# Retention and an x·cos(x) MLP on one core: the first units by head halves, two middle units in coarser chunks

## The chip, the cores and the metric

The kernel runs on one core of a Trainium2 chip. The metric is the device time of one execution in microseconds, and the time of a kernel is the median of its runs. An engine carries out its own instructions in order: TensorE (PE; PEld are its weight loads), VectorE (DVE), ScalarE (ACT), GpSimd (POOL) and SyncE (SP), which issues most of the DMAs.

## The reference

Eight batches of eight heads, 576 positions, head size 64. Attention without a softmax, with a decay by distance, then an MLP on all 4608 tokens:

```python
scores = scale * np.matmul(q, k.transpose(0, 1, 3, 2))
gamma = 1.0 - 2.0 ** (-5.0 - np.arange(H, dtype=np.float32))
Dmat = np.where(rel >= 0, gamma[:, None, None] ** rel[None, :, :], 0.0)
attn = np.matmul(scores * Dmat[None], v)
x = attn.transpose(0, 2, 1, 3).reshape(B * S, H * D)      # 4608 x 512
h = x @ w_in                                              # 512 -> 2048
out = (h * np.cos(h)) @ w_out                             # 2048 -> 512
```

## The kernel before

**Units.** The attention is cut into units `(b, g)`: batch `b`, all eight heads, tokens 256·g to 256·g+255. The last 64 tokens of four batches each make the units `(0, 2)` and `(1, 2)`. The order of units is (0,0), (1,0), (0,1), (1,1), (2,0), (3,0), (2,1), (3,1), (4,0), ..., and two of them (two batches, the same g) make one block of 512 tokens for the MLP, nine blocks in all.

**One unit.** SP loads k, q and v of the unit as float32 into `stgk`, `stgq`, `stgv` (`load`, L484). They are cast to bf16 into `natk`, `qnat`, `natv` (`unit`, L521 for the products with the decay tables `wq`, `wv`; L475 or L474 for the plain casts), with tokens on the partitions. k and q are then transposed into `kt` and `qt`: in blocks 0 and 1 (`NOXBAR`) by TensorE and a copy out of PSUM (`tpe`, L545, copies L474 and L475), in the later ones by a pair of transposing DMAs on SP (`txb`, L560). `scores` multiplies kt and qt within a chunk of tokens on TensorE in four concurrent 64x64 lanes (`emit_lanes`, L591), VectorE multiplies by the triangular mask into `pt` (L630). `states` sums k times v over the chunks in PSUM (`st`), ScalarE copies the sum out (`snap`, into `sba`, `sbb`, `sbr`), and `outputs` adds pt times v and q times the sum of the earlier chunks; two copies bring that into `xt`, the block's MLP input.

A unit is worked in chunks of 64 or of 128 tokens. `fine(u)` says which: fine units (chunks of 64, from batch 2 on, without those in `COARSE`) are loaded in two halves of 128 tokens (256-byte rows), need scores of 64 columns, two pt products and four snaps. The others are loaded whole (512-byte rows), with scores of 128 columns, four pt products and two snaps. Both have the same number of matmuls for the scores and the intra-chunk outputs.

**The first units.** (0,0) and (1,0) are loaded with `fast=True`: q before k before v, each tensor whole, with VectorE casting q, ScalarE and POOL casting a half of k each, and the transposes' copies shared by ScalarE and VectorE. w_in comes in four quarters (`load_w`, issued on POOL, cast to bf16 by the DMA), each gated on a staged tile: quarter 0 on q of (0,0), quarter 2 on q of (1,0), 1 and 3 on k of (1,0). Unit (0,1) is gated on quarter 2. w_out comes in four quarters gated on q of (1,1).

**The MLP.** `mlp1` makes one slice `f` of 128 hidden units for a block or half a block (4 matmuls, L795), ScalarE takes the cosine (L803), VectorE the product into `gt` (L806). `wino2` does the second product in a form with seven instead of eight half-products: VectorE sums of gt and of w_out (L839, L861, L867), TensorE groups `P1`, `P2`, `P6`, `P5`, `P7`, `P3`, `P4` of 16 matmuls (L930), copies and sums (L474, L919), stores (L818).

**The order.** No loop order is written out. `graph` adds tasks with costs in ns and due times (`prio`), and `Graph.run` plans all engines on these costs ahead of time; the resulting order of each engine's instructions is fixed in the program, and each instruction waits for what it needs. `plan` says with which session of which unit the states of which chunk go. Where the planner expects a gap on TensorE in the first 45 us, `warm` puts fillers in: matmuls of a tile of ones (`bk<-one`, L419) whose result is not used. [...]

Of the kernel before, what the change touches and what calls it, by code (L numbers as in the profile page):

```python
# [6 lines left out]
ALU = mybir.AluOpType  # L7
# [12 lines left out]
NT = 72  # L20
# [309 lines left out]
class Kernel:  # L330
# [8 lines left out]
    COARSE = ((2, 0), (3, 0))  # L339
# [138 lines left out]
    def load(self, which, u, rows, gate, fast):  # L478

        stg = self.staged[which, u] = Buf("stg" + which)  # L480
        src = self.src["qkv".index(which)]
        for i, (p0, n, o, ny, b, r0) in enumerate(rows):
            at, w = (b * H * S + r0) * D, ny * D
            self.one("sp", 500, lambda e, p0=p0, n=n, o=o, w=w, at=at: e.dma_start(  # L484
                ap(self.at(stg), 1024, p0, n, o, [w, H], [1, w]), bass.AP(src, at, [[w, n], [S * D, H], [1, w]])),
                r=gate, w=[(stg, i)], sem=lambda i=i: f"{which}{stg.slot}_{i}", dma=1840 if ny == 2 else 600 * n // 64, tail=720 if fast else 1800)
        return stg

    def unit(self, u, fast=False, gate=()):
# [3 lines left out]
        todo = [("k", "natk", "kt"), ("q", "qnat", "qt"), ("v", "natv", None)]  # L493
        for which, nat, dst in [todo[i] for i in ((1, 0, 2) if fast else (0, 1, 2))]:
            if rem:
                rows = [(64 * (b % 2), 64, 512 * (b // 2), 1, 4 * u[0] + b, 512) for b in range(4)]
            elif fine:
                rows = [(0, 128, 512 * y, 1, u[0], 256 * u[1] + 128 * y) for y in range(2)]
            else:
                rows = [(0, 128, 0, 2, u[0], 256 * u[1])]  # L500
            stg = self.load(which, u, rows, gate, fast)
            nb = t[nat] = Buf(nat)
            for y in range(2):
                rs = [(stg, i) for i in ((y,) if fine else range(len(rows)))]
# [9 lines left out]
                if which == "k":  # L514
                    eng = ("act", "pool")[y] if fast else "pool"
                    self.copy(eng, {"act": 520, "dve": 610, "pool": 580}[eng], out, inp, rs, [(nb, y)])
                else:
                    tab, key = (self.WV, "wv") if which == "v" else (self.WQ, "wq")
                    col = 32 if rem else 40 * fine + 16 * u[1] + 8 * y
                    eng = "dve" if fast and which == "q" else "pool"  # L520
                    self.one(eng, 610 if eng == "dve" else 1030, lambda e, out=out, inp=inp, tab=tab, col=col, hs=hs: e.tensor_tensor(  # L521
                        out(), inp(), ap(tab, NT, 0, 128, col, *hs, [0, D]), ALU.mult),
                        r=rs + [(key,)], w=[(nb, y)], port=eng == "pool")
            if dst:
                t[dst] = Buf(dst)
                if self.where(u) in self.NOXBAR:
                    for y in range(2):
                        self.tpe(nb, 512 * y, [(y,)], t[dst], (y,), ("act", "dve")[y] if fast else "act")
        if self.where(u) not in self.NOXBAR:
            self.txb(u)  # L530

    def fine(self, u):
        return u[1] < 2 and u[0] >= 2 and u not in self.COARSE

# [4 lines left out]
    def tpe(self, src, off, rk, dst, wk, eng):  # L539
        bk = Buf("bk")  # L540

        def mm(e):
            tb = self.at(bk).ap().bitcast(BF16)
            for c in range(4):
                inst = e.transpose(tb[:, c * 128:c * 128 + 128],  # L545
                                   ap(self.at(src), 1024, 0, 128, off + 128 * c, [1, 128]), self.IDN.ap())
# [6 lines left out]
        self.copy(eng, dur, lambda: ap(self.at(dst), 1024, 0, 128, off, [1, 512]),  # L553
                  lambda: self.at(bk).ap().bitcast(BF16)[:, 0:512], [(bk,)], [(dst,) + wk])

    def txb(self, u):
# [7 lines left out]
        self.G.add("sp", 2600, parts, dma=3000)  # L564
# [3 lines left out]
    def emit_lanes(self, name, prio, phases, alloc=()):  # L568

        parts, t, n = [], 200, 0  # L570
        for lanes, reads, writes, after in phases:
            lanes = {q: list(v) for q, v in lanes.items() if v}
            order, at = [], dict.fromkeys(lanes, 0.0)
            while any(lanes.values()):
                q = min((q for q in lanes if lanes[q]), key=lambda q: at[q])
                cols, f = lanes[q].pop(0)
                at[q] += cols / 2.4 + 2.5
# [8 lines left out]
            t += max(at.values())  # L586
# [6 lines left out]
    def scores(self, u, prio, todo, split, extra=(), join=None):  # L593
# [5 lines left out]
        for cc in range(1 if rem else 2):  # L599
# [16 lines left out]
            reads = [(x, y) for x in (kt, qt) for y in range(2)]  # L616
# [20 lines left out]
        for i, more in enumerate(extra):  # L637
# [3 lines left out]
            self.emit_lanes("ses=%d.%d" % u, prio + (split or 1000 * (i + 1)), [alone])  # L641
# [200 lines left out]
    def wino2(self, j, base, span):  # L842
# [80 lines left out]
        for n, p in enumerate((1, 2, 6, 5, 7, 3, 4)):  # L923
            l, rr, keys, bank, first = spec[p]
            halves = last and p == 4
            for q in range(2):
# [6 lines left out]
                self.one("pe", 8 * 109, mm, r=keys(0) + keys(1) if halves else keys(q),  # L933
# [159 lines left out]
```

## Time and profile before

| | us |
|---|---|
| median of 3 runs | 291.48 (290.73 to 293.96) |
| the profiled execution | 292.03 |
| its span, first to last instruction | 290.3 |
| TensorE busy | 280.2 (97%) |
| VectorE busy | 209.8 (72%) |
| ScalarE busy | 167.3 (58%) |
| GpSimd busy | 99.7 (34%) |

How to read the lines of the profile: a row of the timeline has its start, its length, engine, line, operation, tile written <- tiles read, shapes, the number of instructions in the row, and in brackets the engine's idle time before it and what ended that. In the DMA lines the last number is the time from issue to landing. In the slices, each digit is the busy share of one fortieth of the span, in tenths. The granted clock of TensorE is full throughout.

### The profile page before, as it was taken

The page shows a single profiled execution, that of the slowest core. Times are in us where ns is not written, and L with a number is a line of the kernel's source. Part 1 is how long each engine was busy: PE and PEld are TensorE (multiplying, and loading weights), DVE is VectorE, ACT ScalarE, POOL GpSimd, SP SyncE. Part 2 cuts the span into 40 slices and gives each one's busy share as a digit, 9 for nine tenths or more (in the row PEclk, how much of TensorE's full clock was granted, in tenths as well). Part 3 has the DMA queues.
Part 4 walks back from the last instruction along what each step waited for, and adds up shares of the span by engine and source line. Part 5 has one row for each costly group of instructions (what it writes and reads, how often), then busy time and mean ns, then how long its engine had stood idle before and what let it go on. Part 6 is the DMA issues. An engine that isn't in the chain of part 4 may idle for free.

```text
span 290.3 us, 9132 instructions
## 1 busy us (share of the span) xinstructions
PE 280.2 (97%) x3848; PEld 192.5 (66%) x3848; DVE 209.8 (72%) x352; ACT 167.3 (58%) x309; POOL 99.7 (34%) x126
## 2 busy tenths in 40 slices
PE   6799999999999999999999999999999999999996
PEld 2566577887864587458566666666666666666685
DVE  3777769999837882897688676878577847667633
ACT  5359786563358634874864766656554483544520
POOL 5451960366650644355174344441430000000000
PEclk9999999999999999999999999999999999999999
DMA  7999899999999999999999999989923000300223
GB/s 200 268 217 281 203 173 219 293 190 197 186 243 199 209 196 248 207 217 281 194 197 181 211 261 212 153 227 197 175 46 146 3 3 0 147 0 0 75 108 108
DMA packets 133127, 49.86 MB, mean 172 GB/s; under 512 B 105440, under 2 KB 128992, under 8 KB 133088
## 3 DMA queue, kind: packets, MB, share of 16 engines
q1 hardware_dynamic: 128576, 44.84, 75.0%
q0 software_dynamic: 4224, 4.19, 9.1%
q8 instruction: 30, 0.49, 0.7%
q10 hardware_dynamic: 288, 0.26, 0.3%
q14 instruction: 9, 0.07, 0.1%
HBM read 36.70 MB, written 9.44 MB: 159 GB/s over the span
## 4 chain that ended last, share of the span: by engine, by line
PE 81%; issue 4%; DVE 4%; DMA 3%; POOL 3%; ACT 2%; SPq 1%; DVEq 0%; POOLq 0%
PE bk L795 37%; PE bk L930 36%; PE bk L591 6%; DMA stgk<-in_k_dram 3%; PE st L591 2%; POOL natv L521 2%; DVE gt L806 2%; ACT cb L803 1%; SPq L484 1%; DVE s L861 1%; DVE pt L630 1%; PE bk L545 1%; POOL win L775 0%; DVE s L867 0%; POOL natk L475 0%
## 5 line engine op out<-in xcount | busy, mean ns | idle before, releaser
L803 ACT ACTIVATE cb<-bk,cpi 128x512 bf16<-128x512 f32 (+1 forms) x168 | 103.5, 627 | 71.0 <-PE bk L795 70.6
L795 PE MATMUL bk<-xt,win 128*128 128x512 bf16 (+1 forms) x672 | 140.5, 349 | 0.6 <-DVE pt L630 0.4
L806 DVE TENSOR_TENSOR gt<-bk,cb 128x512 bf16<-128x512 f32 (+1 forms) x168 | 100.7, 611 | 51.4 <-ACT cb L803 48.4
L795 PEld LDWEIGHTS bk<-xt,win 128*128 128x128 bf16 x672 | 63.9, 98 | 44.0 <-DVE pt L630 0.7
L521 POOL TENSOR_TENSOR qnat<-stgq,wq 128x512 bf16<-128x512 f32 x32 | 33.7, 1065 | 35.2 <-DMA stgq<-in_q_dram 15.0
L521 POOL TENSOR_TENSOR natv<-stgv,wv 128x512 bf16<-128x512 f32 x36 | 38.0, 1069 | 19.0 <-DMA stgv<-in_v_dram 7.4
L475 POOL CAST natk<-stgk 128x512 bf16<-128x512 f32 x34 | 20.2, 611 | 55.9 <-DMA stgk<-in_k_dram 40.3
L930 PE MATMUL bk<-wout,s 128*128 128x256 bf16 x288 | 36.3, 273 | 0.0
L930 PE MATMUL bk<-tw,s 128*128 128x256 bf16 x288 | 35.9, 273 | 0.0
L930 PE MATMUL bk<-wout,gt 128*128 128x256 bf16 x288 | 35.6, 273 | 0.0
L630 DVE TENSOR_TENSOR pt<-bk,tr 128x512 bf16<-128x512 f32 x48 | 30.2, 682 | 4.4 <-PE st L591 2.2
L930 PEld LDWEIGHTS bk<-tw,s 128*128 128x128 bf16 x288 | 28.0, 98 | 7.2
L930 PEld LDWEIGHTS bk<-wout,s 128*128 128x128 bf16 x288 | 27.5, 98 | 6.7
L930 PEld LDWEIGHTS bk<-wout,gt 128*128 128x128 bf16 x288 | 27.7, 98 | 5.4
L919 DVE TENSOR_TENSOR os<-bk,sn 128x512 f32<-128x512 f32 (+1 forms) x28 | 18.5, 664 | 15.0 <-PE bk L930 15.0
L474 ACT ACTIVATE sn<-bk 128x512 f32<-128x512 f32 (+1 forms) x29 | 16.3, 568 | 19.3 <-PE bk L930 19.3
L474 ACT ACTIVATE sba<-st 128x256 bf16<-128x256 f32 x36 | 13.2, 385 | 14.3 <-PE st L591 14.2
L474 ACT ACTIVATE xt<-bk 128x512 bf16<-128x512 f32 x33 | 19.9, 655 | 1.6 <-PE bk L591 1.6
L930 PE MATMUL bk<-tw,gt 128*128 128x256 bf16 x144 | 18.5, 273 | 0.0
L930 PEld LDWEIGHTS bk<-tw,gt 128*128 128x128 bf16 x144 | 13.9, 98 | 4.3
L861 DVE TENSOR_TENSOR s<-gt 128x1024 bf16<-128x1024 bf16 x18 | 15.4, 862 | 0.4
L867 DVE TENSOR_TENSOR s<-gt,s 128x1024 bf16<-128x1024 bf16 x18 | 14.4, 806 | 0.1
(59 smaller groups left out, 171.0 us busy)
## 6 DMA issues: line engine op xcount, KB each, us to landing
out_dram<-os SPq DMA_DIRECT2D x16, 512.0 KB, 4.2
stgk<-in_k_dram SPq DMA_DIRECT2D x20, 256.0 KB, 5.1
stgq<-in_q_dram SPq DMA_DIRECT2D x20, 256.0 KB, 4.9
stgv<-in_v_dram SPq DMA_DIRECT2D x20, 256.0 KB, 5.3
stgq<-in_q_dram SPq DMA_DIRECT2D x6, 512.0 KB, 6.9
stgk<-in_k_dram SPq DMA_DIRECT2D x6, 512.0 KB, 7.7
stgv<-in_v_dram SPq DMA_DIRECT2D x6, 512.0 KB, 7.7
win<-in_moe_w_in_dram POOLq DMA_DIRECT2D x4, 512.0 KB, 8.2
```

Of the source, the lines that this page charges most:

```text
L474: return self.one(eng, dur, lambda e: e.activation(dst(), src(), AF.Copy), r=r, w=w, **kw)
L475: return self.one(eng, dur, lambda e: e.tensor_copy(dst(), src()), r=r, w=w, port=eng == "pool", **kw)
L521: self.one(eng, 610 if eng == "dve" else 1030, lambda e, out=out, inp=inp, tab=tab, col=col, hs=hs: e.tensor_tensor(out(), inp(), ap(tab, ...
L591: return lambda e: e.matmul(out(), lhs(), rhs(), start=start, stop=True, skip_group_check=True)
L630: self.one("dve", 610, lambda e, r=r, b=b, pt=pt: e.tensor_tensor(ap(self.at(pt), 1024, 0, 128, 512 * r, [64 * ny * ny, 8 // ny // ny], [1 ...
L795: inst = e.matmul(ap(self.at(bk), 512, 0, 128, 0, [1, n]), ap(self.WIN, 4 * DFF, 0, 128, c * DFF + 128 * f, [1, 128]), ap(self.at(xt), 204 ...
L803: self.one("act", 70 + n, lambda e: e.activation(ap(self.at(cb), TB, 0, 128, 0, [1, n]), ap(self.at(bk), 512, 0, 128, 0, [1, n]), AF.Sin, ...
L806: self.one("dve", 75 + n / 0.96, lambda e: e.tensor_tensor(ap(self.at(gt), NF * TB, 0, 128, f * TB + 256 * h0, [1, n]), ap(self.at(bk), 51 ...
L861: self.one("dve", 610, lambda e, i=i, q=q, x=x, y=y, op=op: e.tensor_tensor(sv(i, q), x(), y(), op), r=r + late, w=[(S_[i, q],)], port=Tru ...
L867: self.one("dve", 610, lambda e, i=i, q=q, x=x, y=y, op=op: e.tensor_tensor(sv(i, q), x(), y(), op), r=r + late, w=[(S_[i, q],)], port=Tru ...
L919: self.one("dve", 610 if m == 1 else 345, lambda e, i=i, b=b: e.tensor_tensor(view(h, c, i, m), flat(self.at(b), 0, m), flat(self.at(sn[na ...
L930: inst = e.matmul(place(bank, tt), l(f, tt), rr(f), stop=True, skip_group_check=True, start=(first and f == 0 and tt < len(bank)))
```

## The change

Five edits in one:

- `swift` takes the place of `unit(..., fast=True)` for (0,0) and (1,0), and is used for (0,1) as well. It loads, casts and transposes each tensor by head halves (q and k: every second head; v: the first or last four), in the order q, k, q, k, v, v. For (0,1) VectorE casts q (POOL did) and ScalarE copies all transposes. The first scores phase of a unit reads only the first halves. w_in's gates are on the second halves (`GATE`).
- `COARSE` now has (2,1) and (3,1) too: chunks of 128 tokens, loads of whole tiles.
- Fine units load and cast k and v by token halves, and q after them (`ORDER`).
- `plan` moves states to other sessions: the units from (2,0) to (3,1) carry the next unit's first state in their output session, (4,0) (`LINK`) the double set.
- The costs that the planner goes by are set anew (lane sessions, transposing DMAs, due times of the extra sessions).

```diff
-    COARSE = ((2, 0), (3, 0))
+    COARSE = ((0, 0), (1, 0), (0, 1), (1, 1), (2, 0), (3, 0), (2, 1), (3, 1))
...
     def fine(self, u):
-        return u[1] < 2 and u[0] >= 2 and u not in self.COARSE
+        return u[1] < 2 and u not in self.COARSE
...
+        for which, ys in self.ORDER if fine else [(x, (0, 1)) for x in "kqv"]:
...
+    def swift(self, u, gate=()):
...
+        def part(which, a):
+            stg, nb, w = stgs[which], t[nats[which]], 2 * D
+            h0, hn = (4 * a, 1) if which == "v" else (a, 2)
+            at = ((u[0] * H + h0) * S + 256 * u[1]) * D
+            self.one("sp", 500, lambda e: e.dma_start(
+                ap(self.at(stg), 1024, 0, 128, 512 * a, [w, 4], [1, w]),
+                bass.AP(self.src["qkv".index(which)], at, [[w, 128], [hn * S * D, 4], [1, w]])),
+                r=gate, w=[(stg, a)], sem=lambda: f"{which}{stg.slot}_{a}", dma=920, tail=1800 if u[1] else 720)
...
+            eng = self.SWIFTENG[u][which][a]
+            if which == "k":
+                self.copy(eng, {"act": 520, "dve": 610, "pool": 580}[eng], out, inp, [(stg, a)], [(nb, a)])
+            else:
...
+            if which != "v":
+                self.tpe(nb, 256 * a, [(x,) for x in range(a + 1)], t[which + "t"], (a,), self.SWIFTENG[u][which + "t"][a], (512, 2))
+
+        for which, a in self.SWIFTORDER:
+            part(which, a)
...
-        self.G.add("sp", 2600, parts, dma=3000)
+        self.G.add("sp", 2600, parts, dma=3400)
...
-        parts, t, n = [], 200, 0
+        parts, t, n = [], 240, 0
...
-                at[q] += cols / 2.4 + 2.5
+                at[q] += cols / 2.4 + 5
...
-            t += max(at.values())
+            t = max([t] + [parts[i][0] + 200 for i in after if not isinstance(i, Task)]) + max(at.values())
...
-            reads = [(x, y) for x in (kt, qt) for y in range(2)]
+            reads = [(x, y) for x in (kt, qt) for y in range(cc + 1 if u in self.FAST else 2)]
...
+    FAST = ((0, 0), (1, 0), (0, 1))
+    ENG1 = dict(q=("dve", "dve"), k=("act", "pool"), v=("pool", "pool"), qt=("act", "dve"), kt=("act", "dve"))
+    ENG2 = dict(q=("dve", "dve"), k=("pool", "pool"), v=("pool", "pool"), qt=("act", "act"), kt=("act", "act"))
+    SWIFTENG = {(0, 0): ENG1, (1, 0): ENG1, (0, 1): ENG2, (1, 1): ENG2}
+    SWIFTORDER = (("q", 0), ("k", 0), ("q", 1), ("k", 1), ("v", 0), ("v", 1))
+    GATE = (1, 1, 1, 1)
+    RIDE = (4,)
+    LINK = 8
+    ORDER = (("k", (0,)), ("v", (0,)), ("k", (1,)), ("v", (1,)), ("q", (0, 1)))
+
+    def plan(self, seq):
+
+        p = {}
+        for n in range(16):
+            if n > self.LINK and n % 2:
+                p[n] = [[[(n + 1, 0), (n, 3)]], [], [[(n + 1, 1), (n + 2, 0)]]]
+            elif n > self.LINK:
+                p[n] = [[[(n, 2), (n + 1, 1)]], [], [[(n, 3), (n + 1, 2)]]]
+            elif self.fine(seq[n]):
+                p[n] = [[[(n, 0)]], [[(n, 1)], [(n, 2)]], [[(n, 3)]]]
+            elif n in self.RIDE:
+                p[n] = [[[(n, 0)]], [], [[(n, 1)]]]
             else:
...
+                p[n] = [[[]], [[(n, 0)]], [[(n, 1)]]]
+        for n in range(4, self.LINK):
+            if n > 4:
+                p[n] = [[[]], [], p[n][2]]
+            p[n][2][0] += [(n + 1, 0)]
+        n = self.LINK
+        p[n] = [[[(n, 1), (n + 1, 0)]], [[(n, 2), (n + 1, 1)]], [[(n, 3), (n + 1, 2)]]]
...
-            self.load_w("win", x, [(st[which, (min(x, 1), 0)], 0)], pr)
-        self.unit((0, 1), gate=[("win", 2)])
+            self.load_w("win", x, [(st[which, (min(x, 1), 0)], self.GATE[x])], pr)
+        if (0, 1) in self.FAST:
+            self.swift((0, 1), [("win", 2)])
```

## The prediction

> **What bounds the kernel now.** First the page's totals and its slices:
>
> ```profile
> span 290.3 us, 9132 instructions
> PE 280.2 (97%) x3848; PEld 192.5 (66%) x3848; DVE 209.8 (72%) x352; ACT 167.3 (58%) x309; POOL 99.7 (34%) x126
> PE   6799999999999999999999999999999999999996
> DMA  7999899999999999999999999989923000300223
> ```
>
> TensorE is busy 97% of the span, and thin only in the first two slices and the last. But a busy row counts pipelines and fillers. I added up columns instead, from the program's order: columns over 2.4 per ns, a fourth of that for 64x64 tiles, nothing for fillers. That is 250.7 us of real matmul work. So some 40 us of the span are not work: by the timeline's starts about 14 are lost by 20 us, 5 more by 45, 7 more between 45 and 140, 4 more after that. What an edit to the first units can give lies in the first 45 us.
>
> The timeline of the head:
>
> ```profile
> 1.13 3.68 PE L419 MATMUL bk<-one 128*128 128x512 bf16 x9 [1.13 <-DVE lg L445]
> 5.33 0.95 POOL L775 DMA_DIRECT2D win<-in_moe_w_in_dram  x1 [2.23 <-DMA stgq<-in_q_dram]
> 6.71 0.59 PE L419 MATMUL bk<-one 128*128 128x512 bf16 x2
> 9.23 2.48 DVE L630 TENSOR_TENSOR pt<-bk,tr 128x512 bf16<-128x512 f32 x4 [0.61 <-PE bk L591]
> 14.03 1.03 PE L795 MATMUL bk<-xt,win 128*128 128x256 bf16 x8
> 14.72 0.60 POOL L475 CAST natk<-stgk 128x512 bf16<-128x512 f32 x1 [3.14 <-DMA stgk<-in_k_dram]
> 20.01 0.64 PE L591 MATMUL bk<-pt,natv 64*64 64x128 bf16 x32
> 21.06 6.70 PE L795 MATMUL bk<-xt,win 128*128 128x256 bf16 x52
> ```
>
> Unit (0,0) reaches its first MLP matmul at 14.03, unit (1,0) its output matmuls at 20.01, and from 21.06 MLP matmuls follow one another. The DMA issues of the first microseconds give the landings:
>
> ```profile
> stgq<-in_q_dram SPq DMA_DIRECT2D x1, 512.0 KB, 4.2
> win<-in_moe_w_in_dram POOLq DMA_DIRECT2D x1, 512.0 KB, 8.1
> ```
>
> q lands at 0.80 + 4.2 = 5.0; by the same view k at 6.8, v at 8.6, q of (1,0) at 10.4, its k at 14.66 (the weights share the engines), its v at 16.5; w_in's first quarter at 5.33 + 8.1 = 13.4. So whole tiles come 1.8 us apart, a half 0.9.
>
> The timeline behind it, where TensorE is patched with fillers and short gaps:
>
> ```profile
> 27.21 1.16 POOL L475 CAST natk<-stgk 128x512 bf16<-128x512 f32 x2 [8.38 <-DMA stgk<-in_k_dram]
> 32.36 0.38 PE L419 MATMUL bk<-one 128*128 128x512 bf16 x1
> 33.92 0.40 PE L545 MATMUL bk<-idn,natk 128*128 128x128 bf16 x4 [0.25 <-DVE pt L630]
> 34.52 0.40 PE L545 MATMUL bk<-idn,natk 128*128 128x128 bf16 x4 [0.20 <-DVE pt L630]
> 36.92 0.21 PE L591 MATMUL bk<-qt,sba 64*64 64x128 bf16 x1 [0.20 <-issue]
> 44.77 0.61 PE L795 MATMUL bk<-xt,win 128*128 128x256 bf16 x4 [0.37 <-DVE pt L630]
> ```
>
> From 21.06 to the first wino2 group at 42.10 are 21.0 us, and what stands there costs 18.3 back to back (72 MLP matmuls of 256 columns at 0.109, 32 of 512 at 0.216, 32 transposes at 0.053, scores 0.56, states 0.23, an output session 1.06). So 2.7 us are holes.
>
> Last, the later attention sessions and the queues that feed them:
>
> ```profile
> 74.71 1.04 POOL L521 TENSOR_TENSOR natv<-stgv,wv 128x512 bf16<-128x512 f32 x1 [4.24 <-DVE s L867]
> 79.42 2.76 SPq L560 DMA_TRANSPOSE kt<-natk  x1
> 82.23 1.31 SPq L560 DMA_TRANSPOSE qt<-qnat  x1
> 85.96 0.45 PE L591 MATMUL bk<-qt,kt 64*64 64x64 bf16 x32
> 100.69 0.44 PE L591 MATMUL bk<-qt,kt 64*64 64x64 bf16 x32 [0.54 <-POOL natv L521]
> ```
>
> The scores of (2,1) start at 85.96, just as its transposed q lands (82.23 + some 4.4 of the transposes' landing). Sessions are set right behind their data, and one of them pays 0.54.
>
> **The change part by part.**
>
> *Head, (0,0) and (1,0): 0.9 us worse.* In halves, at the landing rate above, q's first half is there at 4.2, k's at 5.0, then 5.9, 6.8, v at 7.7 and 8.6. The last byte comes no sooner. VectorE takes q at 5.9 to 6.6; the second scores need k's second half (POOL 7.1 to 7.7, transposes, VectorE's copy to 8.6) and start at 8.7. Four pt products of 0.65 follow, but the new order puts the cast of (1,0)'s first q half between the third and the fourth, so the last ends at 11.2 (11.7 before) and xt is done at 13.6. This 0.4 us is not collected: w_in's first quarter now waits for q's second half, 0.9 later, and so lands at 14.3. The MLP starts at 14.35 instead of 14.03. (On POOL the cast of k's second half is queued behind that waiting issue; k lands at 6.8, so it loses 0.3, which is in the 7.1.) Unit (1,0): k's second half lands at 14.6 as before, and the transposes queued behind eight MLP matmuls bring the pt products to 17.8 and the outputs to 20.5 (20.0 before). Four MLP matmuls fewer stand ahead of them (16 for 20: 0.44). Together 0.5 + 0.44. If w_in lands as early as before, this is a gain of 0.7; if VectorE waits for q of (1,0) in front of the last pt, the loss is 1.6.
>
> *Unit (0,1), 21 to 42 us: 1.6 better.* Its loads wait for w_in's third quarter as before, which lands at much the same time (its issue moves from 10.8 to 11.3, behind the same first quarter). k landed at 27.1, q at 28.9, v at 30.5; by halves, q first, both q and k are whole at 28.9 and v again at 30.5. What is saved is POOL: two q casts of 1.05 go to VectorE, where MLP products are queued behind them; the first q half lands near 26.2, about when its turn comes, so they do not wait. natv ends at about 31.8 (33.05 before), the first scores come 2 us sooner, the outputs 1.2. In the new order 48 and 36 MLP matmuls of 256 columns stand in this stretch where 44 and 28 stood, so with the four missing ahead of it eight more (0.87) are done by the first wino2 group. I walked through the stretch with the durations above and found 1.1 us of holes (two fillers of 0.2, waits of 0.3 to 0.4 for kt and pt) instead of 2.7. Bounds: all 2.7 gained, or nothing.
>
> *42 to 51 us: nothing.* Unit (1,1) is loaded whole as before, POOL issues w_out and casts behind the same q landing, and VectorE's four pt end the wait at 44.77.
>
> *(2,1) and (3,1) in 128-token chunks: 0.85 worse.* The order's columns add up to 251.5 us instead of 250.7: scores and outputs are twice as wide. The rows agree: 32 scores of 128 columns take 0.58 to the next start, of 64 columns 0.27. This lies on TensorE itself, nothing hides it. VectorE gets four pt more (2.7 us), ScalarE four snaps fewer (1.5). VectorE is 55 to 79% busy from 80 to 100 us and covers them; uncovered they cost 2.7.
>
> *Loads and K, V by halves: 0.25 better.* Between k of (2,0) at 46.8 and the transposes of (4,0) at 99.55 SP sends 6 whole tiles, 21 halves, four pairs of transposes, two stores. After: 12 whole, 10 halves, the same pairs, three stores. Eleven halves at 1.16 (nine in the 10.4 us up to 99.55) go, six tiles at 1.8 and a store of 1.0 come: the transposes start 1.0 sooner, q lands at 105.8 (the added store, queued on SP ahead of them, has its data from some 84 us on). The stall of 0.54 goes, because these scores no longer carry states of (4,0). But q of every later unit is now behind V: two halves and two casts, 4.4 us. In the traced run the scores of (4,0) to (7,0) come 7 to 13 us after q's landing, so that is hidden, except that the planner now sets sessions earlier: by columns (4,0) at 82.4 instead of 89.3, at 107 us. The margin is 1.2 there, 3 at (3,1) and (5,0), and between 2.7 and -0.7 at (2,1). I take 0.3 for stalls, with 4.9 as the upper end (below).
>
> *Tail.* The last 130 rows of TensorE's order are the same.
>
> Sum: +0.9 - 1.6 + 0.85 - 0.54 + 0.3 = -0.1. The profiled execution took 292.03 (span 290.3 and 1.7 around it), so 291.9 for such a one; against the median of the runs, 291.48, it is **291.4**.
>
> **The rivals.**
>
> *The data do come sooner: 288.4.* w_in is in time, the first units lose nothing, all holes from 21 to 42 close (2.7), and the 0.7 around 44.77 as well: -3.4, and -0.54 + 0.85. For it: every filler there marks missing work, and POOL does lose 2.1 us. Against it: the last byte of each unit lands no sooner, and VectorE's pt row of 2.48 stays.
>
> *Sessions set too early: 296.0, slower.* TensorE's queue is in order. In POOL's order both q casts of (2,1) stand behind those of (3,0), in the stretch where POOL waited 4.24 for VectorE. By the cast at 76.4, q would land at 82, and scores are due at 81.3. One more such wait ahead of it makes that 86.2, a stall of 4.9 instead of 0.3. It decides from the point where transposed q lands after 81.3. For it: the margin is the smallest of all. Against it: DMA alone would have q there at 78.6.
>
> *The first fillers are too few: 293.5.* Nine fillers start 0.43 apart, the later pair 0.21: TensorE runs at half rate first, with the granted clock shown full all along. The order now has seven fillers, to 4.1 us, then a pause to 5.0. If that leaves it at half rate up to the MLP, the outputs of (0,0) take 1.05 more (0.7 of it under w_in's landing), transposes and 16 MLP matmuls up to (1,0)'s outputs some 1.7 more: 2.1 in all. [...] Against it: single fillers and transposes follow from 5.0 on.
>
> **How the numbers follow.** 1% (2.9 us) is about what a measurement of this kernel can tell from no change. Chances: the forecast 0.53 (290.0 to 293.2), the sooner data 0.20, the early sessions 0.17, the fillers 0.10. Faster by over 1% is most of the second (0.17), slower most of the third and a little of the fourth (0.18), the rest is within 1%. The range reaches to 288.6 and 294.8, into both outer cases.
>
> **What would show it.** Right: the first MLP matmul at 14.2 to 14.5, the long MLP row from about 21.5, the first wino2 group still near 42 with nine f done instead of seven, no wait for natv near 100. Wrong: that row from 20.5, or transposes of weights twice as far apart before 14 us, or a wait of over 1 us on kt, qt or natv between 60 and 110.

## The result

The kernel after has a median of 292.89 us (291.77 to 294.83, 22 runs), the kernel before, run beside it, 291.42 (290.36 to 293.96, 22 runs). The ratio is 1.0046, with a 95% interval of 1.0027 to 1.0065: 1.34 us slower by the ratio. The forecast was no change that can be measured, 291.4. 292.89 lies within its range, but the change made the kernel slower by more than the uncertainty of this measurement, which is 0.2% to each side and not the 1% that the prediction reckoned with. That the number is near is luck: of its five terms the largest did not come, and a sixth stood at nothing.

The profiled execution of after took 291.97 (span 290.2), 0.9 below its median, that of before 292.03, 0.6 above its own. So the two traces, laid side by side, show no loss at all: where the time went had to come from stages and from further kernels. The page's totals of after, and the slices of the granted clock:

```profile
span 290.2 us, 9057 instructions
PE 280.9 (97%) x3813; PEld 192.9 (66%) x3813; DVE 211.5 (73%) x358; ACT 166.3 (57%) x305; POOL 96.8 (33%) x124
PEclk9799999999999999999999999999999999999999
```

The second digit of PEclk is new: the granted clock was full throughout in the profile of before. By windows of 3.4 us (columns: PE, PEld, DVE, ACT, POOL busy with their counts, then the granted clock, DMA share, GB/s):

```profile
4.26:7.66 3.40, 1.57 (x15) 0.79 (x14) 1.12 (x2) 1.71 (x3) 0.78 (x1) 1.00 1.03 282
7.66:11.08 3.42, 3.22 (x44) 1.53 (x44) 2.62 (x5) 0.00 (x0) 2.84 (x4) 0.50 1.20 277
11.08:14.49 3.41, 2.75 (x80) 1.69 (x79) 2.11 (x5) 1.79 (x4) 0.81 (x1) 1.00 1.19 249
```

TensorE is busy 46% of the window up to 7.66 and then runs at half rate for 3.4 us. One of the prediction's signs of being wrong, transposes twice as far apart before 14 us, is there: four of them take 0.61 at 8.51, where four took 0.40 before. The timeline of the head and of the stretch behind it, with lines of POOL, VectorE and TensorE:

```profile
6.88 0.95 POOL L814 DMA_DIRECT2D win<-in_moe_w_in_dram  x1 [3.77 <-DMA stgq<-in_q_dram]
7.35 0.40 PE L584 MATMUL bk<-idn,qnat 128*128 128x128 bf16 x4 [1.30 <-DVE qnat L562]
8.51 0.61 PE L584 MATMUL bk<-idn,natk 128*128 128x128 bf16 x4 [0.20 <-POOL natk L475]
11.20 0.68 DVE L562 TENSOR_TENSOR qnat<-stgq,wq 128x512 bf16<-128x512 f32 x1
15.00 1.03 PE L834 MATMUL bk<-xt,win 128*128 128x256 bf16 x8 [0.72 <-DMA win<-in_moe_w_in_dram]
21.87 7.14 PE L834 MATMUL bk<-xt,win 128*128 128x256 bf16 x56
27.90 0.69 DVE L562 TENSOR_TENSOR qnat<-stgq,wq 128x512 bf16<-128x512 f32 x1
29.59 0.72 DVE L562 TENSOR_TENSOR qnat<-stgq,wq 128x512 bf16<-128x512 f32 x1
31.37 0.42 PE L630 MATMUL bk<-qt,kt 64*64 64x128 bf16 x16
32.62 1.28 DVE L669 TENSOR_TENSOR pt<-bk,tr 128x512 bf16<-128x512 f32 x2
32.76 1.04 PE L834 MATMUL bk<-xt,win 128*128 128x512 bf16 x4 [0.21 <-DVE gt L845]
43.44 1.03 PE L969 MATMUL bk<-wout,gt 128*128 128x256 bf16 x8
```

The scores of (0,1) and VectorE's products behind them in the kernel before:

```profile
32.70 0.72 PE L591 MATMUL bk<-qt,kt 64*64 64x128 bf16 x32
33.17 2.48 DVE L630 TENSOR_TENSOR pt<-bk,tr 128x512 bf16<-128x512 f32 x4 [0.22 <-PE bk L591]
```

The first MLP matmul comes at 15.00 (14.03 before) and waits for w_in itself, not for `xt`. The two waits for natv at 100.69 and 135.80 are gone, and behind 50 us the view of waits has none for kt, qt or natv.

To compare kernels I set each row's start against the columns of real work ahead of it in the program's order, as in the prediction, at 2.4 columns per ns; the difference is the loss up to there. That rate is a measure: back to back, eight matmuls of 512 columns took 1.73 us in before (199.91 to 201.64), 2.37 columns per ns. Three figures tell most (us):

| profiled execution | long MLP row starts | loss up to it | loss from it to the first wino2 group | loss from there to the end |
|---|---|---|---|---|
| before | 21.06 | 14.87 | 3.55 | 18.14 |
| after | 21.87 | 16.11 | 2.80 | 16.75 |
| after, second profile (e16) | 21.29 | 15.53 | 3.46 | 17.02 |
| fillers in one gap (e1) | 23.06 | 17.30 | 2.56 | 16.74 |
| fine mid units (e3) | 22.68 | 16.92 | 2.47 | 17.69 |
| the first three units whole (e4) | 21.45 | 15.27 | 5.13 | 16.68 |
| (0,1) alone by halves (e7) | 21.25 | 15.06 | 4.01 | 16.38 |
| the same, fine mid units (e8) | 21.41 | 15.23 | 4.01 | 17.45 |
| all gaps filled (e5) | 21.86 | 16.10 | 2.47 | 16.87 |
| the same, second profile (e12) | 22.94 | 17.18 | 2.60 | 16.86 |
| filled, fine mid units (e9) | 21.36 | 15.60 | 3.34 | 18.14 |
| filled further, w_in split (e17) | 21.94 | 16.18 | 2.48 | 17.44 |
| before, fewer fillers (e6) | 21.27 | 15.08 | 2.89 | 17.92 |
| before, (0,1) by halves (e10) | 21.22 | 15.03 | 3.76 | 18.12 |
| before, coarse mid units (e11, e15) | 23.54, 21.37 | 17.35, 15.18 | 3.36, 2.88 | 16.79, 16.84 |

Each row is a single execution. Kernels with the coarse mid units have 251.52 us of columns, the others 250.67, so 0.85 is to be added to their last column before it is compared.

### The profile page after: what moved, and what is told of

Read it like the earlier page. It is cut to its first block, busy times and chain, and to the rows that moved or that the text cites. A ratio compares the mean times of both kernels' runs of the same rounds, so it can differ in the third digit from the quotient of the medians.

```text
span 290.2 us, 9057 instructions
## 1 busy us (share of the span) xinstructions
PE 280.9 (97%) x3813; PEld 192.9 (66%) x3813; DVE 211.5 (73%) x358; ACT 166.3 (57%) x305; POOL 96.8 (33%) x124
## 4 chain that ended last, share of the span: by engine, by line
PE 90%; DMA 4%; DVE 2%; ACT 2%; issue 1%; SPq 0%; DVEq 0%
PE bk L834 43%; PE bk L969 39%; PE bk L630 6%; DMA win<-in_moe_w_in_dram 3%; PE st L630 2%; DMA stgq<-in_q_dram 2%; DVE pt L669 1%; ACT cb L842 1%; DVE gt L845 1%; PE bk L584 0%; ACT kt L474 0%; SPq L546 0%; ACT os L474 0%; DVE tw L878 0%; ACT qt L474 0%
## 5 line engine op out<-in xcount | busy, mean ns | idle before, releaser
L834 PE MATMUL bk<-xt,win 128*128 128x512 bf16 (+1 forms) x672 | 142.6, 349 | 1.4 <-DMA win<-in_moe_w_in_dram 0.7
L522 POOL TENSOR_TENSOR natv<-stgv,wv 128x512 bf16<-128x512 f32 x30 | 31.2, 1046 | 30.5 <-DVE s L900 18.5
L522 POOL TENSOR_TENSOR qnat<-stgq,wq 128x512 bf16<-128x512 f32 x30 | 31.2, 1052 | 28.8 <-DVE s L906 20.5
L969 PE MATMUL bk<-wout,gt 128*128 128x256 bf16 x288 | 36.8, 273 | 0.0
L969 PE MATMUL bk<-tw,s 128*128 128x256 bf16 x288 | 36.5, 273 | 0.0
L475 POOL CAST natk<-stgk 128x512 bf16<-128x512 f32 x34 | 21.0, 628 | 45.7 <-DVE s L906 16.2
L669 DVE TENSOR_TENSOR pt<-bk,tr 128x512 bf16<-128x512 f32 x52 | 33.4, 682 | 3.4 <-PE bk L630 2.3
L958 DVE TENSOR_TENSOR os<-bk,sn 128x512 f32<-128x512 f32 (+1 forms) x28 | 18.4, 664 | 8.1 <-PE bk L969 8.0
L474 ACT ACTIVATE sba<-st 128x256 bf16<-128x256 f32 x32 | 11.8, 385 | 13.2 <-PE st L630 13.0
L900 DVE TENSOR_TENSOR s<-s,gt 128x1024 bf16<-128x1024 bf16 x18 | 13.1, 731 | 0.2
L906 DVE TENSOR_TENSOR s<-gt,s 128x1024 bf16<-128x1024 bf16 x18 | 13.0, 729 | 0.2
```

Source lines behind the costliest of these rows:

```text
L474: return self.one(eng, dur, lambda e: e.activation(dst(), src(), AF.Copy), r=r, w=w, **kw)
L475: return self.one(eng, dur, lambda e: e.tensor_copy(dst(), src()), r=r, w=w, port=eng == "pool", **kw)
L522: self.one("pool", 1030, lambda e, out=out, inp=inp, tab=tab, col=col, hs=hs: e.tensor_tensor(out(), inp(), ap(tab, NT, 0, 128, col, *hs, ...
L669: self.one("dve", 610, lambda e, r=r, b=b, pt=pt: e.tensor_tensor(ap(self.at(pt), 1024, 0, 128, 512 * r, [64 * ny * ny, 8 // ny // ny], [1 ...
L834: inst = e.matmul(ap(self.at(bk), 512, 0, 128, 0, [1, n]), ap(self.WIN, 4 * DFF, 0, 128, c * DFF + 128 * f, [1, 128]), ap(self.at(xt), 204 ...
L900: self.one("dve", 610, lambda e, i=i, q=q, x=x, y=y, op=op: e.tensor_tensor(sv(i, q), x(), y(), op), r=r + late, w=[(S_[i, q],)], port=Tru ...
```

## Experiments

Theory A: idle stretches in the head let the clock fall. Theory B: w_in, gated on q's second half, is late and TensorE waits for it. Theory C: the wider chunks of (2,1) and (3,1) cost their columns.

**Fillers in one gap (e1).** The order of all engines stays; the third place of fillers gets five more.

```diff
-                    self.warm(max(1, self.G.fill(gap, warm)))
+                    self.nw = getattr(self, 'nw', 0) + 1; self.warm(max(1, self.G.fill(gap, warm)) + {3: 5}.get(self.nw, 0))
```

> The kernel after, order of every engine unchanged, with five more fillers on TensorE in its idle stretch from 6.05 to 7.35 us. Theory A (the granted clock, half from 8 to 11 us in the profile and on average 0.982 to 1.0 from run to run, is most of the 1.4 us lost): the clock is full in every run and the time about 292.2, ratio to before 1.002 to 1.003. Theory B (w_in's first quarter lands 1.5 us later, and MLP matmuls wait for it): the clock is full too, but what becomes faster ends before w_in lands, so 292.9 and 1.0046 stay. Theory C (the wider scores and outputs of the two mid units): 292.9 as well.

293.03, ratio 1.0056 [1.0031, 1.0081]: nothing gained. But the fall of the clock had moved, not gone. In this profile it is behind the next gap, in which TensorE waited 1.30 for w_in:

```profile
11.22:14.63 3.41, 1.82 (x62) 1.12 (x59) 1.62 (x3) 2.10 (x5) 0.81 (x1) 1.00 1.17 256
14.63:18.03 3.40, 3.39 (x21) 2.71 (x22) 1.17 (x3) 1.50 (x3) 2.61 (x4) 0.52 1.12 218
```

And the time goes with it: the four runs at a mean clock of 0.999 to 1.0 have a median of 291.95, the four at 0.993 to 0.994 one of 293.78.

**w_in sooner (e2).** The issue keeps its place on POOL and waits for the first halves of q.

```diff
-                ops.append(self.P.add(t.eng, fn, r=[phys(k) for k in r],
+                r = [(b, 0) for b, x in r] if w and w[0] in (('win', 0), ('win', 2)) else r; ops.append(self.P.add(t.eng, fn, r=[phys(k) for k in r],
```

> The kernel after, order of every engine unchanged, but the first two quarters of w_in wait for the first half of q of (0,0) and of (1,0) instead of the second. Theory B: the first quarter lands near 12.5 to 13.5, the first MLP matmul comes at 14.1 to 14.3 instead of 15.0, set by VectorE's products and xt, and the time falls by 0.5 to 0.7 to about 292.3. Theory A: the clock still falls at 8 us; a gain of 0.2 at most. Against both: the weights then share the DMA engines with v of (0,0) and with q of (1,0), which land up to 1.8 later, and (1,0)'s outputs come no sooner than 20.8; then the time stays at 292.9.

295.93, 1.0145 [1.0120, 1.0169], worse than either theory had it. Timeline of VectorE and TensorE:

```profile
13.18 0.69 DVE L562 TENSOR_TENSOR qnat<-stgq,wq 128x512 bf16<-128x512 f32 x1 [2.15 <-DMA stgq<-in_q_dram]
13.93 0.40 PE L584 MATMUL bk<-idn,qnat 128*128 128x128 bf16 x4 [2.41 <-DVE qnat L562]
14.62 1.07 PE L630 MATMUL bk<-pt,natv 64*64 64x128 bf16 x32 [0.29 <-DVE pt L669]
```

w_in is issued at 4.14 (6.88 in after), and tiles issued behind it land later: the first half of q of (1,0) at 13.2 (10.2 in after). Its cast stands on VectorE ahead of the last pt product of (0,0), and the outputs of (0,0) come at 14.62 instead of 12.63, at half clock.

**The mid units fine again (e3).**

```diff
-    COARSE = ((0, 0), (1, 0), (0, 1), (1, 1), (2, 0), (3, 0), (2, 1), (3, 1))
+    COARSE = ((0, 0), (1, 0), (0, 1), (1, 1), (2, 0), (3, 0))
-    LINK = 8
+    LINK = 6
```

> The kernel after with (2,1) and (3,1) back in chunks of 64 tokens (their session chain as before the change); the head and the rest keep the change's form, and TensorE's order is the same up to the scores of (2,0) near 70 us. Theory C: 0.85 us of columns go, 292.0, ratio 1.002, unless waits for natv or qt (0.54 and 0.28 in the kernel before) come back, which would leave 292.6. Theories A and B alone: the gain is what columns say, not more, so at least 0.5 of the loss stays. If the mid units are all of the loss, the ratio is 1.000.

292.14, 1.0037 [1.0015, 1.0058]: 0.26 less by the ratios. But the clock fell in five of these 12 runs too; the runs at full clock alone (a mean clock of 0.999 or more) have a median of 291.47, those of after one of 292.12. By these C costs 0.65, most of the 0.85 of its columns.

**The first three units whole (e4).** `swift` gets the body of the old `load` and `unit`, the halves' one is called `halves`.

```diff
-    def swift(self, u, gate=()):
+    def halves(self, u, gate=()):
...
+    def swift(self, u, gate=()):
+        rem, fine, fast = False, False, u[1] == 0
...
```

> The kernel after with the first three units loaded, cast and transposed as whole tiles, as before the change (their planned durations too); the mid units and the K, V loads keep the change's form. Theories A and B together put 1.25 us of the loss in the head (0.8 by the start of the long MLP row, 0.44 by four MLP matmuls fewer ahead of it), and 0.5 given back by 43 us: 291.8 to 292.2, with the full clock in every run. If only C holds: 292.9 or more, since eight MLP matmuls fewer are done by the first wino2 group.

292.83, 1.0054 [1.0041, 1.0066], not faster: the rest of the change, planned around whole tiles, is as slow as the change itself. In its profile the loss lies between the long row and the first wino2 group, 5.13 (3.55 before): at 39.40 two fillers and a wait of 0.70 for xt cost 1.44. The planner put a new order together for these units, so this run does not tell the whole tiles from the order around them.

**All gaps filled (e5, e12), and before with fewer fillers (e6).** The edit of e1 with `{3: 5, 7: 5, 10: 3}` on after, and with `{1: -2, 2: -2, 6: -2}` (and no call for 0) on before.

> The kernel after, order of every engine unchanged, with thirteen more fillers on TensorE: five in the idle stretch before the transposes at 7.35, five ahead of the first MLP matmul (idle 13.3 to 14.6 with the first five alone, and the half rate then fell on 14.6 to 18.5), three ahead of the output matmuls of (1,0). Theory A (idle stretches in the head let the granted clock fall to half for some microseconds, at a moment that differs from run to run): the mean clock is 0.999 or 1.0 in every run, none is above 292.5, and the median is that of the runs at full clock, 291.7 to 292.0. Rival (the clock has its own reasons, the fillers don't matter): clocks from 0.982 to 1.0 and 292.9 as before.

292.18, 1.0024 [1.0001, 1.0047], and a mean clock of 0.999 or more in all of the 12 runs; of the 22 runs of after, 16 were below. So full clock came as said; the times still reach to 294.1. By the ratios the clock costs 0.64 us.

> The kernel before, order unchanged, with six fillers fewer in the head: seven instead of nine at the start, none at 6.71, none at 12.91. Theory A: TensorE is as thinly used as after the change, the clock falls to half somewhere between 7 and 20 us in most runs, mean clock 0.982 to 0.994, and the time rises by 0.5 to 2 us to 292 to 293.3 with the same work. Rival: clock 1.0 and 291.3, the same as before.

292.09, 1.0020 [1.0002, 1.0039]. Only four of 12 runs were below 0.998, and they were not the longer ones: the fillers taken out don't decide it. In its profile the clock is at half for one window from some 7.3 us on, under waits for data, and the long row still starts at 21.27. The fall in the profile of after cost nothing either: after and e5 both have the first MLP matmul at 15.00 and the long row at 21.87 and 21.86. That of e1, behind w_in's landing, put it at 23.06. So in these profiles a fall cost time where TensorE had work queued.

> The kernel with thirteen more fillers once more, for a second profile, since its runs at full clock reach from 291.5 to 294.1 and the one profiled was among the fastest (291.8). If what differs are stalls of TensorE in the sessions from 60 us on: in a run near 292.5 they show as waits of 0.3 to 0.7 there. If it differs in the head: the long MLP row starts later than in the first profile.

292.97, and of the 1.2 more than in e5 1.08 are lost in the head, at full clock:

```profile
16.07 1.03 PE L834 MATMUL bk<-xt,win 128*128 128x256 bf16 x8 [1.20 <-DMA win<-in_moe_w_in_dram]
```

From there on the two traces run alike (16.87 and 16.86 behind the first wino2 group). In six profiles of after's loads (after, e1, e3, e5, e12, e16) the first MLP matmul starts when w_in lands, at 14.42 to 16.07. In the kernel before it lands at 13.4 and the matmuls start 0.6 later, at 14.03, for other reasons. In none of the eight profiles with whole tiles there (before, e4, e6, e7, e8, e10, e11, e15) do they wait for w_in; they start at 13.99 to 14.62: there such a spread is covered.

**(0,1) alone by halves, then with fine mid units (e7, e8).** From e4, with

```diff
-            self.swift((0, 1), [("win", 2)])
+            self.halves((0, 1), [("win", 2)])
```

> The kernel after with (0,0) and (1,0) as whole tiles as before the change, and only (0,1) by head halves; mid units and K, V halves as in the change. The prediction's terms: the 0.9 lost in the first two units goes, the 1.6 of the stretch from 21 to 42 us stays, so 290.5 by the terms, and with what the clock took 291.0 to 291.5 (ratio 0.997 to 1.001), the first wino2 group at 42.0 with 36 MLP matmuls of block 1 done, full clock. Rival (the halves of (0,1) gain nothing over whole tiles): 292.8 as with all three units whole.

> As the run before it, and (2,1) and (3,1) back in chunks of 64 tokens. If the parts add up: another 0.3 (what the finer chunks alone gave in ratio) to 0.85 (their columns) less, 290.2 to 291.0, faster than both kernels. Rival: the sessions planned 0.8 us later wait for natv or qt again (0.54 and 0.28 in the kernel before), and it equals the run before it.

292.76, 1.0037 [1.0017, 1.0056], full clock in 12 of 12 runs; and 291.83, 1.0017 [0.9994, 1.0040]. The head's 0.9 is back in the profile (loss of 15.06 up to the long row), the 1.6 is not there: 4.01 from the long row to the first wino2 group, 3.55 before. The rival of e7 held. e8 took 0.58 less than e7 by the ratios, the step that the first reading gave to the chunks, but from e7's level: it isn't faster than before.

**Both costs away (e9), and single parts on the kernel before (e10, e11, e15).** e9 is e5 with the edit of e3. In e10 and e11 the planner's costs, `ORDER`, `RIDE` and the head are as before; e10 has `halves` for (0,1) alone, e11 the wider `COARSE` and `LINK = 8` alone.

> The kernel after with both suspected costs taken away: the thirteen more fillers in the head, and (2,1) and (3,1) in chunks of 64 tokens. If the clock (0.7 us by the run with all gaps filled) and the chunks (0.7 by the finer chunks alone) are two separate costs and together the whole loss: full clock in every run and 291.4 to 291.7, ratio 0.999 to 1.001. Rival (the head itself also loses what it loses in the profile, 0.4 by 55 us): 291.9, ratio 1.0015 or more.

291.72, 1.0012 [0.9988, 1.0036]: with fillers and fine chunks the loss is not to be told from none.

> The kernel before with one part of the change alone: (0,1) loaded, cast and transposed by head halves. The prediction's term for 21 to 42 us (1.6, bounds 0 and 2.7) would make it 289.8 to 291.4. The profile of the mixed kernel stands 0.4 ahead of before at 55 us, so 291.0 by that, ratio 0.9985. Rival (the later sessions give the lead back, since their loads do not come sooner): 291.5, ratio 1.000.

292.38, 1.0029 [1.0009, 1.0048]: alone, the halves of (0,1) make the kernel before slower.

> The kernel before with one part of the change alone: (2,1) and (3,1) in chunks of 128 tokens; loads, planned durations and head as before. Columns 251.5 instead of 250.7, so +0.85; the wait of 0.54 for natv near 100 us goes or stays. By the prediction's terms 291.7 to 292.3, ratio 1.001 to 1.003; if VectorE's four more products are not hidden, or the sessions wait for natv more often, 293 or more.

292.69, 1.0048 [1.0020, 1.0077]: alone, the coarse mid units cost 1.4 by the ratio, the largest single part. Its profile had the clock fall too, with the head of before:

```profile
20.39 0.44 PE L630 MATMUL st<-natv,natk 64*64 64x64 bf16 x16 [1.95 <-POOL natv L1146]
```

> The kernel before with only the chunks of (2,1) and (3,1) widened, a second profile, since the first had its clock at half in the head. If the 1.2 us are columns (0.85) and small waits behind 60 us, then from there to the end it takes 15.8 to 16.5 us over the pure column time of the narrower chunks, where the kernel before took 16.1 in its profile and some 15.5 in its median run. If it is chance in the head: the long MLP row starts after 21.5 again.

291.35, the long row at 21.37. From 60 us to the end it lost 14.8, with the 0.85 of columns 15.6: under the 15.8 to 16.5 said, and before had 16.1. This profile shows no cost of C, where the timed runs of e11 at full clock alone have a median of 292.54, 1.23 above those of before beside them (291.31).

**w_in in two halves (e13), with the other two measures (e14), and more fillers (e17).** The first quarter is issued as 256 columns at its place and 256 behind the next POOL task; only f of 2 and 3 wait for the latter.

```diff
-        self.one("pe", 4 * (n / 2.4 + 2.6), mm, r=[("win", f // 4)] + self.xkeys(j, ses),
+        self.one("pe", 4 * (n / 2.4 + 2.6), mm, r=[("win", f // 4)] + [("winb",)] * (f in (2, 3)) + self.xkeys(j, ses),
...
+            if t.eng == "pool" and self.half and getattr(self, "due", 0): self.P.add("pool", self.half, w=["winb"], sem="winb"); self.half = None
```

> The kernel after, order of every engine unchanged, but the first quarter of w_in is loaded as two halves of 256 columns: the first at its place, the second issued on POOL behind the cast of k's second half of (0,0); the MLP matmuls of the first two f blocks need only the first half. If w_in's landing is what the head loses: the first half lands near 13.5, the first MLP matmul comes at 14.0 to 14.3 instead of 15.0, set by xt, and the median falls by 0.6 to 0.9 to 292.0 to 292.3. Rival (the added issue of 0.95 on POOL holds back v's products, or the second half lands after 16 us): nothing won, 292.9.

292.57, 1.0039 [1.0014, 1.0063]: 0.2 by the ratios.

```profile
14.08 1.05 PE L836 MATMUL bk<-xt,win 128*128 128x256 bf16 x8 [0.47 <-ACT xt L476]
16.26 1.05 PE L836 MATMUL bk<-xt,win 128*128 128x256 bf16 x8 [0.68 <-DMA win<-in_moe_w_in_dram]
```

The first MLP matmul came at 14.08, set by xt, as said; the second eight then waited for the second half, and the long row started at 21.82, as in after. The wait was moved, not removed.

> The three measures together: thirteen fillers more, chunks of 64 tokens in (2,1) and (3,1), and w_in's first quarter in two halves. From 291.7 with the first two, another 0.6 to 0.9 less: 290.8 to 291.1, ratio 0.998, faster than both kernels if it holds. Rival (as above): 291.7.

292.04, 1.0038 [1.0005, 1.0070]. The six runs at full clock have a median of 291.27, the other six one of 294.35. Its profile is one of the latter; below it the same window of e17, which has eight fillers more (`{3: 8, 5: 5, 7: 5, 10: 3}`):

> The kernel with all three measures (fillers, chunks of 64 tokens, w_in's first quarter in two halves) and eight fillers more: three in the stretch before the second transposes of q, five ahead of the states of (0,0), where its profile had TensorE idle 1.1 us and busy 1.89 of the 3.41 us before its clock fell at 11.65. Theory A: no window of 3.4 us is much under two thirds busy, so no run is below a mean clock of 0.998, and the median is that of the full-clock runs of the kernel without these eight, 291.3 (ratio 0.999). Rival (the clock falls for another reason, or the fillers hold back the matmuls behind them): clocks of 0.988 again in half the runs and 292 or more.

```profile
8.24:11.65 3.41, 1.89 (x39) 0.85 (x39) 3.29 (x6) 0.00 (x0) 3.39 (x5) 1.00 1.15 246
11.65:15.05 3.40, 3.33 (x78) 2.67 (x79) 1.18 (x2) 1.02 (x3) 1.24 (x3) 0.51 1.23 240
15.05:18.46 3.41, 3.41 (x10) 1.36 (x11) 1.31 (x2) 1.45 (x3) 2.54 (x4) 0.50 1.22 220
```

```profile
8.24:11.65 3.41, 3.04 (x49) 1.51 (x46) 3.41 (x7) 0.00 (x1) 2.22 (x3) 1.00 1.26 248
11.65:15.05 3.40, 3.40 (x72) 2.23 (x71) 1.43 (x3) 2.47 (x5) 0.91 (x2) 1.00 1.26 249
```

e17: 291.60 (291.20 to 292.12), 1.0012 [0.9999, 1.0024], 0.999 or more in all 12 runs. With the thin stretch filled (3.04 of 3.41 busy instead of 1.89) the clock stayed full, and the runs lie within 0.9 us. It isn't faster than before: no kernel here was.

> The kernel after once more, for a second profile: the first (291.97) was below its median of 292.89. If the head differs from run to run (w_in's landing, then the clock), the long MLP row starts after 21.9, and what follows from there to the end is equal to the first profile within 0.3. If stalls behind 60 us differ, they show there as waits.

292.34 at full clock, w_in at 14.42 after a wait of 1.51, the long row at 21.29, sooner than in the first profile and not later. What follows is equal within 0.3 behind the first wino2 group, but 0.66 slower ahead of it, 0.54 of that one wait for nothing but the issue at 36.80.

## Why the prediction was wrong, step by step

*Head, 0.9 worse: right in size up to the long row.* Five profiles with halves and full clock (e5, e9, e12, e16, e17) lose 16.12 up to the long row on average, six with whole tiles and full clock there (before, e4, e7, e8, e10, e15) 15.11: 1.01. The landings were taken as fixed, and they vary. In the first profile of after q's second half landed at 6.55, not 5.9, and k's at 7.5, not 6.8; w_in was issued at 6.88 and the first MLP matmul came at 15.00, not 14.35. In e9 and e16 q's second half came at 5.9 as said, and the first MLP matmul at 14.48 and 14.42. The case "VectorE waits for q of (1,0) in front of the last pt, the loss is 1.6" is what e2 brought about.

*21 to 42 us, 1.6 better: the step that failed.* The stretch to the first wino2 group gained 0.75 in the profiled pair; on average 2.81 was lost in eleven profiles with the head and (0,1) in halves, 3.11 in three with both whole and the order of before (before, e6, e15): 0.30. The prediction moved the casts to VectorE, "where MLP products are queued behind them", had them find their data in time, "so they do not wait", and priced the delay of what is queued at nothing. Before, VectorE had idle times of 0.17 to 0.76 ahead of each gt product there, waiting for ScalarE. After, w_in's third quarter was issued at 13.06, not 11.3, but (0,1)'s loads started at 19.39 (19.13 before), as said. q's first half landed at 25.5, but its cast waited in VectorE's queue until 27.90. The casts (27.90, 29.59) have taken the idle times, the row is without a gap up to 31.6, and the pt products start at 32.62 (33.17 before) although the first scores start 1.3 sooner, at 31.37. TensorE waits for VectorE's gt at 32.76, and that wait with the filler ahead of it costs 0.59, in e5 as well. The outputs came 0.3 sooner (35.64), not 1.2, and the first wino2 group at 43.44, not near 42. The prediction counted POOL's 2.1 us as gained, when they were moved to an engine that TensorE waits for.

The queue is not the whole of it. In e7 the first cast starts at 26.30, when its data land, and the outputs come at 33.95, 2.0 sooner than before; up to them 2.14 is lost, where before lost 2.44 and e6 and e15 2.02 and 2.03. So even outputs that come sooner than forecast leave the holes as large: TensorE's waits for kt, gt and pt move with the session. Behind the outputs e7 loses 1.88, before 1.11. Up to the first wino2 group the kernels with (0,1) whole have lost 18.0 to 18.4 (before, e6, e15), those with (0,1) alone in halves 18.8 to 19.2 (e7, e8, e10), the five with the head in halves too 19.0 on average. The head and this stretch together, -0.7 in the sum, came to +0.8, and (0,1) by halves brings that alone. The order is planned anew in each of these kernels; what share it has in this is open.

*42 to 51 us, nothing: right.* From the end of the first wino2 group to the one behind (1,1)'s outputs 1.63 was lost before, 1.71 after.

*Mid units and loads, 0.61 worse (0.85 - 0.54 + 0.3): right in sign; the chunks cost their columns.* Timed, the chunks cost 0.26 (after against e3), 0.35 (e5, e9), 0.58 (e7, e8) and 1.40 us (e11 against before), all by ratios, 0.65 on average. The medians of the runs at full clock alone differ by 0.65, 0.51, 0.97 and 1.23 in these four pairs, 0.84 on average; the columns are 0.85. The waits near 100 and 136 went, as said. But in the profiled executions the kernels with coarse units have 16.38 to 17.38 of loss behind the first wino2 group, those with fine ones 17.2 to 18.14; with the columns added this is no difference. Why the timed runs differ and the profiled ones don't is open.

*The clock: in the sum it is nothing, and it costs 0.6 to 0.7.* After to e5 is 0.64, e3 to e9 0.73. The prediction named a rival near it (fillers too few, 293.5, chance 0.10), but as a start that stays at half rate up to the MLP, and no run shows that. In the trace of before the eighth filler, of 0.50, spans the change to the full rate, and the ninth, from 4.42, takes 0.38. After's seven fillers reached the full rate at 4.25, as the four transposes at 4.75 show, which take 0.40 (the slices count the time before the change as full). The start was at half rate for longer in other profiles, with seven fillers (to some 6 us in e16, 7.14 in e13) and with nine (6.23 in e15), and the long row came no later for it (21.29, 21.82, 21.37). What cost time are falls later in the head. What the prediction set against the rival, "single fillers and transposes follow from 5.0 on", is where TensorE was busy 1.57 us of the 3.40 ahead of the fall. The mean clock of a run tells how often it fell: 3.4 us at half rate are 1.7 of 290 us, 0.006, so 0.994, 0.988 and 0.982 are one, two and three windows, and the profiled runs bear it out (0.994 for 3.41 us in after, e1, e6 and e11, 0.988 for 6.83 in e3 and e14, 0.982 for both in e2).

*Sessions set too early, 296.0: did not happen.* No wait on qt at (2,1).

By the timed runs, fillers and fine chunks together (after to e9) take away 0.99 of the 1.34; the 0.35 left (1.0012) is not to be told from none. So the clock and the columns are the loss that can be shown, and the 0.94 that the sum had as gained from everything else (0.9 - 1.6 - 0.54 + 0.3) did not come. The 0.8 that the profiles lose by the first wino2 group does not show in full in the median: its share in the 0.35 is open, since the profiles are single executions.

## What to carry to other kernels

When a cast moves to another engine, cost it by what is queued behind it there; VectorE, with idle times of 0.17 to 0.76 us ahead of dependent products, had no room for two casts of 0.7. Data that come sooner are worth the waits that they end; here outputs 2.0 sooner ended almost none. With 0.6 us of cover behind its landing in before, w_in delayed the first MLP matmul in none of the eight profiles with whole tiles; behind the later half of q the whole spread of its landing (14.42 to 16.07 in six) delayed it. And where one profiled execution of each kernel agrees with the other and the medians don't, sort the runs by their mean granted clock before explaining rows: the price of the chunks came out of the runs at full clock.

## What the runs showed of the hardware

In these profiles the clock fell by whole windows of 3.41 us. While matmuls run, seven profiles show eight falls: 3.41 us at half rate in five (after, from 7.66 to 11.08; e1, e6, e11, the first of e2), 6.83 in a row in three (e3, e14, the second of e2). All changes of the clock within a profile lie whole multiples of 3.41 us apart. On the grid that they give, TensorE was busy 1.00 to 1.82 us of the 3.41 just ahead of each fall (29 to 53%; e1 1.82, e14 1.81, whose rows above begin 0.09 off this grid). No window that was busy for 1.84 or more at full rate was followed by a fall, in any of the 16 profiles that show a change: the least busy ones are 1.84 (e11, from 4.06), 1.90 (before, from 4.33) and 1.92 (e9, from 7.27). The ends of matmuls are modelled, so by estimate these times are good to about a tenth. So in its profile before, with its fillers, was hardly busier (1.90) than the busiest window ahead of a fall (1.82). Where the grid lies differs from profile to profile (falls begin at 7.66 in after, 8.57 in e3, 11.74 in e14, 21.13 in e11), so that the same thin stretch falls into one window or is shared by two; that would explain why a kernel's clock falls in some runs and not in others. What makes a fall last two windows isn't shown: in e14 TensorE was busy through all of the first, from 11.74 on (3.33 of the 3.40 us in the row above). The longest idle times in the windows ahead of the falls were 1.1 (e14) to 2.4 us (e2).

Loads in halves landed less evenly in these profiles. Rate in half microseconds of the first 20 us of after:

```profile
GB/s 0 0 0 16 62 304 344 320 177 199 241 313 320 318 334 306 296 288 292 284 271 225 223 204 213 218 259 294 330 325 302 220 204 190 199 205 195 207 205 205
```

From 4.0 to 5.5 it has 177, 199 and 241, where whole tiles have 334, 293 and 289 in the same view of before. The mean of this stretch is 182 (e12) to 261 in ten profiles with the head in halves and w_in gated on q's second half, 305 to 317 in eight with whole tiles. The issue of w_in, which waits for q of (0,0), came at 6.14 to 7.35 in the former, at 5.22 to 5.63 in the latter. Why the rate drops isn't shown. And TensorE now and then waits 0.3 to 0.8 us for nothing but the issue, in places that differ from profile to profile (0.54 at 36.80 in e16, 0.82 at 53.95 in e10, 0.56 and 0.59 at 104.90 and 120.87 in e8), which no term of the sum had.
